# Attention and routed experts on one core: the first loads in half heads on two queues, wider idle products, and VectorE for the second pair's copies

## The chip, the cores and the metric

The kernel runs on one core of one Trainium2 chip. The metric is the device time of one execution in microseconds, as a median over runs. The profile below comes from one execution with the hardware profiler on; its times count from the start of the profiled span.

## The reference

Two blocks are chained. The first is windowed attention for 4 batches, 8 heads, 768 positions and a head size of 64; the second sends each of the 3072 resulting rows of 512 to one of 8 experts. All numbers are float32. Cut to what matters:

```python
scores = scale * np.matmul(q, k.transpose(0, 1, 3, 2))
is_global = pos[None, :] < int(n_global)               # n_global = 8
is_local = (rel >= 0) & (rel < int(n_local))           # n_local = 96
dist = np.where(is_global & ~is_local, float(n_local), np.abs(rel))
scores = np.where(is_global | is_local, scores - slopes * dist, -1e9)
a = np.exp(scores - max); a = a / sum(a)
x = (a @ v) laid out as 3072 rows of 512
expert_idx = argmax(cosine(x, expert_emb) / tau)       # the gate is the softmax value there
out[rows of e] = gate * (relu(x @ w1[e]) @ w2[e])      # 512 -> 1024 -> 512
```

`n_global` and `n_local` are inputs, so the kernel has to load these two numbers before it can build its table of bias factors.

## The kernel before, in words

**Attention.** A group is four heads of one batch, so there are eight groups; a group holds two pairs of heads. For a pair, `k` and `q` are loaded with positions on the partitions (`load_tokens`, L420, one DMA for a head) and turned on TensorE (`turn`, L455: three transposes into one PSUM bank, then copies to `kT` or `qT` by ScalarE, L457, L460 and L462). `turn(t, i)` takes half of `k` (i of 0 and 1) or half of `q` (i of 2 and 3). The 768 positions are cut into eight blocks of 96, each with the first 30 positions beside it as possible global columns. A unit is one block of a group: `score` (L480) makes its scores for four heads in two PSUM banks, `grow` (L486, ScalarE) takes the exponential, `weigh` (L493, VectorE) multiplies by the table, `attend` (L509 for the values, L519 for the sums) multiplies by `v`. A step has two units, so a group has four steps, and the attention of a step is issued one step later.

**The start.** All of group 0 is loaded at once. SyncE issues the first halves of `k` (L420, four DMAs of 96 KB), ScalarE those of `q`; then SyncE alone issues the second halves of `q`, the values (`load_v`, L426, four DMAs of 192 KB; L429, one of 30 KB for the global rows, which GpSimd spreads to the other blocks, L430), the second halves of `k`, two small loads for the router (L140, L142) and then group 1. The two numbers come in by two DMAs that GpSimd issues (`load_numbers`, L109). VectorE turns them into values (L112 to L117), builds the distances (`window_table`, L353 to L368), and ScalarE makes the table from them (L373, four instructions for four heads). VectorE also clears the five PSUM banks (L701). `busy(n)` (L706) issues n products of a matrix of ones, whose result nobody reads; a float32 product is two records in the trace. They stand ahead of the first turns and between them.

**What sets the order.** In this part the order on TensorE, ScalarE, VectorE and SyncE is the order of the program text, GpSimd's is the planner's. Each DMA of SyncE and ScalarE takes the next of eight semaphores in turn, so the issue of a DMA waits until the eighth DMA before it has landed. SyncE issues in order: what waits holds up all that follows.

**The rest.** After the eight groups come routing, gathers and the experts. The change doesn't touch them.

Of the kernel before, what the change touches and what calls it, by code (L numbers as in the profile page):

```python
# [10 lines left out]
I32 = mybir.dt.int32  # L11
# [9 lines left out]
P = 128  # L21
# [10 lines left out]
BLK = 96  # L32
GLB = 30
BAND = 32
ROWS = BLK + GLB
NB = 8
# [67 lines left out]
def load_numbers(k, n_global, n_local):  # L104

    nc, pool = k.nc, k.const
    raw = pool.tile([P, 2, 2], I32, name="raw")
    for i, ap in enumerate((n_global, n_local)):
        nc.gpsimd.dma_start(raw[:, i, :], ap.bitcast(I32).partition_broadcast(P))  # L109
    yield  # L110
    words = pool.tile([P, 2, 2], F32, name="words")
    nc.vector.tensor_copy(out=words[:], in_=raw[:])  # L112
# [264 lines left out]
def window_attention(k, ctx):  # L377
# [3 lines left out]
    nc, tc, NT, D, B, S, H, E = k.nc, k.tc, k.NT, k.D, k.B, k.S, k.H, k.E  # L381
# [18 lines left out]
    banks = [pa_p.tile([P, 512], F32, name="pa%d" % i) for i in range(5)]  # L400
    turn_of = [0]

    def bank():
        turn_of[0] += 1
        return banks[turn_of[0] % len(banks)]
# [8 lines left out]
        t.kT = kt_p.tile([P, NB, P], F32, name="kT", tag="kT")  # L414
        return t

    def load_tokens(eng, dst, src, b, a, r0, r1):

        for e in range(2):
            eng.dma_start(dst[:, r0:r1, e, :],  # L420
                          src[b, 2 * a + e].rearrange("(t p) d -> p t d", p=P)[:, r0:r1, :])

    def load_v(g, hs):
        for h in hs:
            src = k.v[g.b, 4 * g.m + h]
            nc.sync.dma_start(g.v[0:BLK, h], src.rearrange("(j r) d -> r j d", r=BLK))  # L426

        h0, h1 = hs[0], hs[-1] + 1
        nc.sync.dma_start(g.v[BLK:ROWS, h0:h1, 0], k.v[g.b, 4 * g.m + h0 : 4 * g.m + h1, 0:GLB].rearrange("h r d -> r h d"))  # L429
        nc.gpsimd.tensor_copy(out=g.v[BLK:ROWS, h0:h1, 1:], in_=g.v[BLK:ROWS, h0:h1, 0:1].to_broadcast([GLB, h1 - h0, NB - 1, D]))  # L430

    def new_group(b, m):
        g = Net()
# [6 lines left out]

    def load_part(g, p):
        if p < 2:
            load_tokens(nc.sync, g.pairs[p].k, k.k, g.b, 2 * g.m + p, 0, NT)
            load_tokens(nc.sync, g.pairs[p].q, k.q, g.b, 2 * g.m + p, 0, NT)
        else:
            load_v(g, (2 * p - 4, 2 * p - 3))

    def turn(t, i):  # L450

        src, half = (t.k, t.q)[i // 2], i % 2
        ps = bank()
        for r in range(3):
            nc.tensor.transpose(ps[:, r * P : (r + 1) * P], src[:, 3 * half + r, :, :], k.ident[:])  # L455
        if i < 2:
            nc.scalar.copy(out=t.kT[:, 4 * half : 4 * half + 4, 0:BLK],  # L457
                           in_=ps[:, 0 : 3 * P].rearrange("d (j c) -> d j c", c=BLK))
        else:
            nc.scalar.copy(out=t.qT[:, 3 * half * P : 3 * (half + 1) * P], in_=ps[:, 0 : 3 * P])  # L460
        if i == 0:
            nc.scalar.copy(out=t.kT[:, :, BLK:ROWS], in_=t.kT[:, 0:1, 0:GLB].to_broadcast([P, NB, GLB]))  # L462

    def score(u):

# [221 lines left out]
    first = groups[0]  # L687
    open_group(first)
    numbers = load_numbers(k, k.n_global, k.n_local)
    next(numbers)  # L690
    build_consts(k)
    for a in range(2):
        load_tokens(nc.sync, first.pairs[a].k, k.k, 0, a, 0, 3)
        load_tokens(nc.scalar, first.pairs[a].q, k.q, 0, a, 0, 3)
    warm = const.tile([P, 1], F32, name="warm")
    nc.scalar.activation(warm[:], k.ones[:, 0:1], AF.Exp)
    for a in range(2):
        load_tokens(nc.sync, first.pairs[a].q, k.q, 0, a, 3, NT)

    for ps in banks:  # L700
        nc.vector.memset(ps[:], 0.0)  # L701
    idle = bank()

    def busy(n):
        for _ in range(n):
            nc.tensor.matmul(idle[:, 0:64], lhsT=k.ones[:], rhs=k.ones[:, 0:64], start=True, stop=True)  # L706

    busy(8)
    load_v(first, range(4))
    for a in range(2):  # L710
        load_tokens(nc.sync, first.pairs[a].k, k.k, 0, a, 3, NT)
    emb = prep_expert_emb(k, k.emb_in, k.tau, tmp)
    next(emb)
    open_group(groups[1])
    for p in range(4):
        load_part(groups[1], p)
# [3 lines left out]
    next(table)  # L720
    next(numbers)
    next(table)
    check_numbers(k)
    build_route_consts(k)


# [870 lines left out]
def kernel(  # L1597
# [40 lines left out]
    with ExitStack() as moe:  # L1638
# [9 lines left out]
        with tc.manual_schedule(engines=ORDERED), ExitStack() as inner:  # L1648
            window_attention(n, inner)
# [130 lines left out]
```

## Time and profile before

| | |
|---|---|
| median of 3 runs | 523.97 us (522.73 to 524.47) |
| profiled execution, its own time | 524.56 us |
| its span | 522.8 us |
| TensorE busy, share of the span | 500.1 us, 96% |
| VectorE, ScalarE, GpSimd busy | 301.8 us, 197.2 us, 153.7 us |
| TensorE busy from 0 to 20 us | 15.55 us |
| HBM read, written | 61.66 MB, 17.16 MB |

The span runs from the first to the last instruction of the profiled execution, 1.8 us less than its own time. TensorE has work in nearly all of it. The first 20 us are the exception: its busy time there includes the idle products, and the loads of group 0 arrive in this time.

### The profile page before, as it was taken

How to read it: one execution, taken by the hardware profiler on the slowest of the kernel's cores; microseconds unless marked ns; L12 is line 12 of the kernel's file. 1: busy time of each engine (PE TensorE's matmuls, PEld its weight loads, DVE VectorE, ACT ScalarE, POOL GpSimd, SP SyncE). 2: the span in 40 equal slices, each digit the busy share in tenths (PEclk: the TensorE clock that was granted, in tenths of full speed). 3: DMA queues.
4: the chain of work that ended last, by engine and by line, in shares of the span. 5: the costliest groups of instructions: out<-in, count | busy, mean ns of one | idle time of the engine just before them, and what ended most of it. 6: DMA issues, size and time to landing. Idle time of an engine off the chain costs nothing.

```text
span 522.8 us, 13699 instructions
## 1 busy us (share of the span) xinstructions
PE 500.1 (96%) x5606; PEld 411.3 (79%) x5606; DVE 301.8 (58%) x602; ACT 197.2 (38%) x493; POOL 153.7 (29%) x169
## 2 busy tenths in 40 slices
PE   7899999999988998999999999999999999999995
PEld 7677887887765787859878759989889789859964
DVE  5647667666685664756745606765646644715531
ACT  4867766766653411302322312412312222302210
POOL 4221121442544235354240024144053050013023
PEclk9999999999998999999999999999999999999999
DMA  9999998898443346817573018357056064001001
GB/s 169 200 188 181 220 261 207 212 229 177 104 103 92 94 102 118 265 56 287 195 284 118 2 44 296 150 197 263 3 217 242 4 224 163 1 16 67 0 22 67
DMA packets 111421, 76.32 MB, mean 146 GB/s; under 512 B 87077, under 2 KB 95269, under 8 KB 111281
## 3 DMA queue, kind: packets, MB, share of 16 engines
q1 hardware_dynamic: 102769, 59.00, 42.1%
q0 software_dynamic: 6912, 15.26, 8.8%
q8 instruction: 63, 1.03, 0.9%
q14 instruction: 77, 0.63, 0.4%
q10 hardware_dynamic: 1600, 0.39, 0.3%
HBM read 61.66 MB, written 17.16 MB: 151 GB/s over the span
## 4 chain that ended last, share of the span: by engine, by line
PE 67%; issue 18%; DVE 3%; POOL 3%; ACT 3%; DMA 3%; SPq 1%; POOLq 1%; ACTq 0%; DVEq 0%
PE big L1303 17%; PE big L1108 9%; PE od L509 7%; PE pa L480 5%; PE work L1236 4%; PE od L519 3%; PE pa L455 3%; PE work L1108 3%; PE work L1249 3%; PE pa L671 2%; PE work L1017 2%; POOL out_dram L1255 2%; PE big L1279 2%; PE pa L582 2%; PE work L1027 1%
## 5 line engine op out<-in xcount | busy, mean ns | idle before, releaser
L493 DVE TENSOR_TENSOR ex<-ex,table 126x768 f32<-126x768 f32 x64 | 61.3, 964 | 45.1 <-ACT ex L486 44.9
L1315 DVE TENSOR_TENSOR hT<-big,hT 128x320 f32<-128x320 f32 (+4 forms) x70 | 39.4, 566 | 49.9 <-PE big L1303 49.7
L1255 POOL DMA_INDIRECT out_dram<-y_arm,tids x17 | 17.1, 1004 | 167.4 <-ACT y_arm L1238 121.1
L486 ACT ACTIVATE ex<-pa 126x384 f32<-126x384 f32 (+1 forms) x128 | 53.3, 477 | 24.4 <-PE pa L480 18.6
L1303 PE MATMUL big<-xT,w1t 128*128 128x160 f32 (+4 forms) x336 | 59.4, 330 | 1.1 <-issue 1.1
L1303 PEld LDWEIGHTS big<-xT,w1t 128*128 128x128 f32 x336 | 54.2, 190 | 3.9 <-issue 2.0
L991 POOL DMA_INDIRECT xg<-x_dram,idss x32 | 35.4, 1106 | 42.9 <-PE big L1303 21.5
L509 PE MATMUL od<-ex,v 126*64 126x192 f32 (+1 forms) x576 | 47.0, 309 | 0.0
L480 PE MATMUL pa<-qT,kT 64*32 64x128 f32 (+4 forms) x2048 | 41.0, 263 | 3.7 <-issue 3.5
L480 PEld LDWEIGHTS pa<-qT,kT 64*32 64x32 f32 (+1 forms) x2048 | 30.2, 105 | 16.7 <-issue 12.3
L257 POOL DMA_INDIRECT meta<-mt,slot x24 | 27.2, 1133 | 49.9 <-DVE rd L553 20.9
L509 PEld LDWEIGHTS od<-ex,v 126*64 126x64 f32 x576 | 35.3, 139 | 7.9 <-issue 3.8
L1303 PE MATMUL big<-xsum,fsum 128*128 128x160 f32 (+4 forms) x224 | 39.6, 330 | 0.0
L1020 ACT COPY xT<-work 128x256 f32<-128x256 f32 x56 | 18.1, 375 | 56.0 <-PE work L1017 55.3
L1303 PEld LDWEIGHTS big<-xsum,fsum 128*128 128x128 f32 x224 | 36.1, 190 | 1.2
L1236 PE MATMUL work<-w2t,hT 128*128 128x512 f32 x80 | 35.1, 594 | 0.0
L1108 PE MATMUL big<-wsum,hsum 128*128 128x256 f32 x136 | 31.1, 380 | 1.1 <-issue 0.6
L1317 ACT ACTIVATE hT<-hT 128x320 f32<-128x320 f32 (+4 forms) x42 | 21.6, 533 | 25.5 <-DVE hT L1315 25.3
L430 POOL COPY v<-v 30x896 f32<-30x896 f32 (+1 forms) x15 | 18.4, 1239 | 41.1 <-DMA v<-in_v_dram 28.9
L1108 PEld LDWEIGHTS big<-wsum,hsum 128*128 128x128 f32 x136 | 25.7, 190 | 5.6 <-issue 1.4
L1236 PEld LDWEIGHTS work<-w2t,hT 128*128 128x128 f32 x80 | 15.1, 190 | 17.7 <-issue 17.6
L1113 DVE TENSOR_TENSOR ptmp<-big,ptmp 128x256 f32<-128x256 f32 x16 | 6.7, 421 | 38.0 <-PE big L1108 20.0
(246 smaller groups left out, 899.8 us busy)
## 6 DMA issues: line engine op xcount, KB each, us to landing
w1t<-in_moe_w_dram SPq DMA_DIRECT2D x6, 2048.0 KB
w2t<-in_moe_w_dram SPq DMA_DIRECT2D x6, 2048.0 KB
v<-in_v_dram SPq DMA_DIRECT2D x32, 192.0 KB
x_dram<-xs SPq DMA_DIRECT2D x23, 256.0 KB
k<-in_k_dram SPq DMA_DIRECT2D x28, 192.0 KB
q<-in_q_dram SPq DMA_DIRECT2D x28, 192.0 KB
w1t<-in_moe_w_dram SPq DMA_DIRECT2D x32, 128.0 KB
w2t<-in_moe_w_dram SPq DMA_DIRECT2D x32, 128.0 KB
```

Of the source, the lines that this page charges most:

```text
L257: i = nc.gpsimd.indirect_dma_start(out=k.meta[:], out_offset=bass.IndirectOffsetOnAxis(ap=slot[:, t : t + 1], axis=0), in_=mt[:, t, :], in ...
L480: i = nc.tensor.matmul(u.sp[e][k0:k1, a * n + c0 : a * n + c1], lhsT=t.kT[rows, j, k0:k1], rhs=t.qT[rows, j * BLK + c0 : j * BLK + c1], st ...
L486: nc.scalar.activation(u.ex[:, e], u.sp[e][0:ROWS, 0 : 2 * u.n].rearrange("p (a c) -> p a c", a=2), AF.Exp, scale=k.scale)
L493: nc.vector.tensor_tensor(out=exv, in0=exv, in1=tab[:, :, 0 : u.n // BLK, :], op=ALU.mult)
L509: nc.tensor.matmul(g.od[a][e * D : (e + 1) * D, at : at + c1 - c0], lhsT=g.v[0:ROWS, 2 * a + e, u.j, :], rhs=u.ex[:, e, a, c0:c1], start=f ...
L991: i = k.nc.gpsimd.indirect_dma_start(out=xg[:], out_offset=None, in_=k.x_dram[0 : upto or k.N + 1, :], in_offset=bass.IndirectOffsetOnAxis ...
L1108: i = self.k.nc.tensor.matmul(ps, lhsT=x[:, f, :], rhs=w[:, f, :], start=f == 0 and not add, stop=True, skip_group_check=True)
L1236: nc.tensor.matmul(ps[:], lhsT=hT[:, f, j * P : (j + 1) * P], rhs=w2[:, f, :], start=i == 0, stop=i == k.NF - 1)
L1255: i = k.nc.gpsimd.indirect_dma_start(out=k.out.rearrange("t (i m) -> (t i) m", i=n), out_offset=bass.IndirectOffsetOnAxis(ap=ids, axis=0), ...
L1303: nc.tensor.matmul(to[f // 2][:, f % 2 * 256 : f % 2 * 256 + h], lhsT=x[:, l, f * P : (f + 1) * P], rhs=y[:, l, 0:h], start=not (add or f ...
L1315: nc.vector.tensor_tensor(out=to, in0=x, in1=z, op=ALU.add)
L1317: nc.scalar.activation(to, to, AF.Relu)
```

## The change

- The two numbers are loaded by one DMA on SyncE and one on ScalarE, as the first of each queue, and no longer by GpSimd.
- The first halves of `k` and `q` come in the order k, q of pair 0, then k, q of pair 1, with one head of each on SyncE and the other on ScalarE. Before, SyncE had all of `k` and ScalarE all of `q`.
- The values of group 0 are loaded in two parts: blocks 0 to 3 (four DMAs of 96 KB) and the global rows ahead of the second halves of `k`, blocks 4 to 7 behind them. The spread of the global rows on GpSimd has two parts too.
- The five clears of PSUM banks are gone.
- The idle products have 256 columns and no longer 64; there are 7, 3 and 2 of them, and no longer 8, 3 and 3.
- VectorE and no longer ScalarE makes the three copies of the second pair's first turns; `check_numbers` comes behind them.

```diff
-    for i, ap in enumerate((n_global, n_local)):
-        nc.gpsimd.dma_start(raw[:, i, :], ap.bitcast(I32).partition_broadcast(P))
+    for i, (eng, ap) in enumerate(((nc.sync, n_global), (nc.scalar, n_local))):
+        eng.dma_start(raw[:, i, :], ap.bitcast(I32).partition_broadcast(P))
...
-    def load_tokens(eng, dst, src, b, a, r0, r1):
+    def load_tokens(engines, dst, src, b, a, r0=0, r1=NT):
         for e in range(2):
-            eng.dma_start(dst[:, r0:r1, e, :],
-                          src[b, 2 * a + e].rearrange("(t p) d -> p t d", p=P)[:, r0:r1, :])
+            engines[e % len(engines)].dma_start(dst[:, r0:r1, e, :],
+                                                src[b, 2 * a + e].rearrange("(t p) d -> p t d", p=P)[:, r0:r1, :])
-    def load_v(g, hs):
+    def load_v(g, hs, j0=0, j1=NB):
...
-            nc.sync.dma_start(g.v[0:BLK, h], src.rearrange("(j r) d -> r j d", r=BLK))
+            nc.sync.dma_start(g.v[0:BLK, h, j0:j1], src.rearrange("(j r) d -> r j d", r=BLK)[:, j0:j1])
...
-    def turn(t, i):
+    def turn(t, i, copy=nc.scalar.copy):
...
-    for a in range(2):
-        load_tokens(nc.sync, first.pairs[a].k, k.k, 0, a, 0, 3)
-        load_tokens(nc.scalar, first.pairs[a].q, k.q, 0, a, 0, 3)
+    for a, t in enumerate(first.pairs):
+        load_tokens((nc.sync, nc.scalar), t.k, k.k, 0, a, 0, 3)
+        load_tokens((nc.sync, nc.scalar), t.q, k.q, 0, a, 0, 3)
...
-    for ps in banks:
-        nc.vector.memset(ps[:], 0.0)
     idle = bank()
     def busy(n):
-        for _ in range(n):
-            nc.tensor.matmul(idle[:, 0:64], lhsT=k.ones[:], rhs=k.ones[:, 0:64], start=True, stop=True)
-    busy(8)
-    load_v(first, range(4))
-    for a in range(2):
-        load_tokens(nc.sync, first.pairs[a].k, k.k, 0, a, 3, NT)
+        for i in range(n):
+            nc.tensor.matmul(idle[:, i % 2 * 256 : i % 2 * 256 + 256], lhsT=k.ones[:],
+                             rhs=k.ones[:].unsqueeze(1).to_broadcast([P, 2, P]), start=True, stop=True)
+    busy(7)
+    load_v(first, range(4), 0, NB // 2)
+    for a, t in enumerate(first.pairs):
+        load_tokens((nc.sync,), t.k, k.k, 0, a, 3, NT)
+    load_v(first, range(4), NB // 2, NB)
...
-    check_numbers(k)
     build_route_consts(k)
...
     busy(3)
-    turn(first.pairs[1], 0)
-    turn(first.pairs[1], 2)
+    turn(first.pairs[1], 0, nc.vector.tensor_copy)
+    turn(first.pairs[1], 2, nc.vector.tensor_copy)
     next(table)
-    busy(3)
+    check_numbers(k)
+    busy(2)
```

More of the change, by code (lines that the diff above doesn't have):

```diff
@@ L415, in new_pair @@
         return t
[L417 removed]
+    def load_tokens(engines, dst, src, b, a, r0=0, r1=NT):
         for e in range(2):
[L420 to L423 removed]
+            engines[e % len(engines)].dma_start(dst[:, r0:r1, e, :],
+                                                src[b, 2 * a + e].rearrange("(t p) d -> p t d", p=P)[:, r0:r1, :])
+    def load_v(g, hs, j0=0, j1=NB):
         for h in hs:
             src = k.v[g.b, 4 * g.m + h]
[L426 removed]
+            nc.sync.dma_start(g.v[0:BLK, h, j0:j1], src.rearrange("(j r) d -> r j d", r=BLK)[:, j0:j1])
         h0, h1 = hs[0], hs[-1] + 1
[L429 to L430 removed]
+        if j0 == 0:
+            nc.sync.dma_start(g.v[BLK:ROWS, h0:h1, 0], k.v[g.b, 4 * g.m + h0 : 4 * g.m + h1, 0:GLB].rearrange("h r d -> r h d"))
+        j0 = max(j0, 1)
+        nc.gpsimd.tensor_copy(out=g.v[BLK:ROWS, h0:h1, j0:j1], in_=g.v[BLK:ROWS, h0:h1, 0:1].to_broadcast([GLB, h1 - h0, j1 - j0, D]))
     def new_group(b, m):
@@ L442, in load_part @@
         if p < 2:
-            load_tokens(nc.sync, g.pairs[p].k, k.k, g.b, 2 * g.m + p, 0, NT)
-            load_tokens(nc.sync, g.pairs[p].q, k.q, g.b, 2 * g.m + p, 0, NT)
+            load_tokens((nc.sync,), g.pairs[p].k, k.k, g.b, 2 * g.m + p)
+            load_tokens((nc.sync,), g.pairs[p].q, k.q, g.b, 2 * g.m + p)
         else:
             load_v(g, (2 * p - 4, 2 * p - 3))
-    def turn(t, i):
+    def turn(t, i, copy=nc.scalar.copy):
         src, half = (t.k, t.q)[i // 2], i % 2
@@ L456, in turn @@
         if i < 2:
-            nc.scalar.copy(out=t.kT[:, 4 * half : 4 * half + 4, 0:BLK],
-                           in_=ps[:, 0 : 3 * P].rearrange("d (j c) -> d j c", c=BLK))
+            copy(out=t.kT[:, 4 * half : 4 * half + 4, 0:BLK],
+                 in_=ps[:, 0 : 3 * P].rearrange("d (j c) -> d j c", c=BLK))
         else:
-            nc.scalar.copy(out=t.qT[:, 3 * half * P : 3 * (half + 1) * P], in_=ps[:, 0 : 3 * P])
+            copy(out=t.qT[:, 3 * half * P : 3 * (half + 1) * P], in_=ps[:, 0 : 3 * P])
         if i == 0:
-            nc.scalar.copy(out=t.kT[:, :, BLK:ROWS], in_=t.kT[:, 0:1, 0:GLB].to_broadcast([P, NB, GLB]))
+            copy(out=t.kT[:, :, BLK:ROWS], in_=t.kT[:, 0:1, 0:GLB].to_broadcast([P, NB, GLB]))
     def score(u):
@@ L691, in window_attention @@
     build_consts(k)
-    for a in range(2):
-        load_tokens(nc.sync, first.pairs[a].k, k.k, 0, a, 0, 3)
-        load_tokens(nc.scalar, first.pairs[a].q, k.q, 0, a, 0, 3)
+    for a, t in enumerate(first.pairs):
+        load_tokens((nc.sync, nc.scalar), t.k, k.k, 0, a, 0, 3)
+        load_tokens((nc.sync, nc.scalar), t.q, k.q, 0, a, 0, 3)
     warm = const.tile([P, 1], F32, name="warm")
     nc.scalar.activation(warm[:], k.ones[:, 0:1], AF.Exp)
-    for a in range(2):
-        load_tokens(nc.sync, first.pairs[a].q, k.q, 0, a, 3, NT)
-    for ps in banks:
-        nc.vector.memset(ps[:], 0.0)
+    for a, t in enumerate(first.pairs):
+        load_tokens((nc.sync,), t.q, k.q, 0, a, 3, NT)
     idle = bank()
     def busy(n):
-        for _ in range(n):
-            nc.tensor.matmul(idle[:, 0:64], lhsT=k.ones[:], rhs=k.ones[:, 0:64], start=True, stop=True)
-    busy(8)
-    load_v(first, range(4))
-    for a in range(2):
-        load_tokens(nc.sync, first.pairs[a].k, k.k, 0, a, 3, NT)
+        for i in range(n):
[3 more added lines that the diff above has]
+    load_v(first, range(4), 0, NB // 2)
+    for a, t in enumerate(first.pairs):
+        load_tokens((nc.sync,), t.k, k.k, 0, a, 3, NT)
+    load_v(first, range(4), NB // 2, NB)
     emb = prep_expert_emb(k, k.emb_in, k.tau, tmp)
```

## The prediction

> **What bounds the kernel now.** The page's busy times come first: TensorE 96%, so only a stretch in which it idles or does nothing useful can be won, and the change edits the first 20 us. The chain that ended last, in order of time (start, length, what), shows whose work counts there:
>
> ```profile
> 1.89 5.11 DMA q<-in_q_dram
> 7.00 0.02 issue
> 7.02 0.34 SPq L426
> ...
> 12.03 4.60 DMA k<-in_k_dram
> 16.63 0.14 issue
> 16.76 0.52 PE pa L455 x3
> 17.28 1.45 PE od L509 x16
> 18.73 0.71 PE pa L480 x19
> 19.44 1.24 ACT ex L486 x3
> ```
>
> The start is a chain of loads, not of products: SyncE can't issue the first values (L426) before a first half of `q` has landed at 7.00, the second halves of `k` are behind the values in its queue and land at 16.63, and TensorE's turn at 16.76 waits for them. From 19.44 ScalarE is the bound until 26.8 (it is busy 5.97 of the 6.00 us from 20 to 26), from 27 TensorE. From 27 us to the end of attention the waits name no load of `k` or `q` ahead of TensorE, so a lead at 27 us is kept.
>
> Why do loads issued by 2.94 land at 7.0? Busy time by stretch (PE, PEld, DVE, ACT, POOL, then clock, DMA share, GB/s):
>
> ```profile
> 2.50:3.50 1.00, 1.00 (x5) 1.00 (x5) 0.94 (x2) 0.53 (x1) 0.97 (x5) 1.00 1.22 270
> 3.50:5.50 2.00, 2.00 (x11) 2.00 (x11) 0.94 (x4) 0.96 (x2) 1.86 (x10) 1.00 0.60 112
> 5.50:7.50 2.00, 2.00 (x12) 2.00 (x12) 0.84 (x5) 0.61 (x2) 1.83 (x16) 1.00 1.17 233
> ```
>
> With work queued, the rate falls from 270 to 112 GB/s and comes back. In the trace's packets the fall starts with the first packet of GpSimd's queue (the two numbers, 3.3 us) and ends with its last (6.0 us). That is coincidence in time, not proof.
>
> The timeline shows the other engines:
>
> ```profile
> 2.50 3.68 PE L706 MATMUL pa<-ones 128*128 128x64 f32 x16 [2.50 <-DVE pa L701]
> 5.97 0.85 PE L455 MATMUL pa<-ident,k 128*128 128x128 f32 x3
> 6.52 0.17 DVE L112 CAST words<-raw 128x4 f32<-128x4 int32 x1 [1.54 <-DMA raw<-in_n_local_dram]
> 10.06 0.56 DVE L368 TENSOR_TENSOR w_rel<-w_rel,w_t 128x384 f32<-128x384 f32 x1
> 10.71 1.76 ACT L373 ACTIVATE table<-w_rel 128x384 f32<-128x384 f32 x4
> 12.38 1.23 ACT L486 ACTIVATE ex<-pa 126x384 f32<-126x384 f32 x3
> 15.93 0.52 PE L455 MATMUL pa<-ident,k 128*128 128x128 f32 x3 [0.70 <-DMA k<-in_k_dram]
> 20.10 0.82 PE L455 MATMUL pa<-ident,q 128*128 128x128 f32 x6
> ```
>
> Pair 0's `k` landed at 4.17 and `q` at 4.45 (semaphore updates in the trace), yet the turn starts at 5.97: the idle products stand ahead of it. The first exponential waits until 12.38, behind a table that waits for the numbers. Group 1's second `q` landed at 19.94, and the turn at 20.10 takes it at once.
>
> **What the Trainium skill says.** "TensorE: Matmul & The Clock Gate", Part 1: the array runs at half clock until about a busy window of 3.4 us has passed, and windows run free of the kernel's start. The trace agrees: a transpose record lasts 421 ns before 9.5 us and 272 later, and the products' pace changes from 213 to 112 ns at 9.8 us. "DMA: Bandwidth & Descriptors", "Issuing engines are not separate DMA queues": a second issuing engine saves issue time only; here that is 0.49 us for 96 KB. The same page, "SWDGE vs HWDGE vs iDMA": software rings and hardware queues share the engines, which take turns between them; the dip above is consistent with that.
>
> **The change part by part.**
> *Clears* (five, 2.65 us of VectorE): gone. TensorE's first product waits only for `ones`, done at 1.08, so it starts at 1.1 and no longer at 2.50.
>
> *Idle products.* A warm record of 256 columns takes 216 ns start to start (L1108 in the trace); cold is twice that, 430. busy(7) is 14 records: 6.0 us cold. Before, 16 records took 3.47. When does the clock come on? Counting back windows of 3.41 from 9.82 gives edges at 6.41 and 2.99; the window between them held 64-column products, which fill half of the array time, and did not switch the clock. With 256 columns it is full, so I take 6.4. Ends: 4.5 with a lucky phase, 9.8 if the width doesn't matter. With 6.4: busy(7) ends at 6.8; two turns at 6 x 0.107 = 0.64 to 7.4; busy(3) 6 x 0.216 = 1.3 to 8.7; two turns to 9.35; busy(2) 0.86 to 10.2. Scores start at 10.2 against 10.47, a gain of 0.3 only (9.2 and 11.9 at the ends).
>
> *Numbers first.* Two more DMAs, one on each queue: 0.5 us of delay for the rest of each queue; ScalarE's fifth DMA now waits for the first number, with its table load and the copies (from 6.86 before) behind it, and 1.5 us of room. They should land near 3. The iotas on GpSimd come 1.3 us sooner (its two issues, 0.73 and 0.58, are gone), so L353 runs at 3.3 and the VectorE stretch of 4.1 us (6.52 to 10.62) ends near 7.8.
>
> *Copies.* ScalarE loses 0.48 + 0.39 + 0.47 = 1.34 us. VectorE gets three; a 128x384 copy from PSUM is 0.55 on VectorE (L525), so about 1.45 with the spread: from 9.2 to 10.7, where ScalarE finished at 10.59. Queued behind are `check_numbers` (0.5) and the first `weigh`, which is not due before 12. The table (1.76) runs at 8.6 to 10.4 and no longer at 10.71 to 12.47. So the first exponential starts when the first unit is scored, near 11.2 against 12.38: 1.2 us sooner.
>
> *Order of the loads.* Ahead of the second halves of `k` now lie 393 + 31 KB of values and not 786 + 31; at the 203 GB/s of 7.5 to 14 us that is 1.9 us. Without the dip another 1.5 or so. I estimate them at 12 to 13, against 16.63; TensorE asks for them near 13.5, so this wait is gone, and what is late next is bank and exponential on ScalarE. The first attention then starts near 14.9 (before 17.21), the scores of step 2 wait for ScalarE's copies, and ScalarE reaches step 2's exponentials near 17.4 against 19.42: **2.0 us**.
>
> *What that runs into.* The bytes up to group 1 are the same, but SyncE has 24 issues ahead of it and not 19: +5 x 0.5 = 2.5 us, against which its two waits (2.85 to 3.71 and 5.67 to 7.02, 2.2 us) should vanish. First issue of group 1 near 13.7, before 13.45; with less queued ahead of it, the second `q` should land near 18.5, before 19.94. TensorE would take it at 17.9, so it loses 0.6 there; but before, ScalarE came to step 3's exponentials at 24.88, 0.6 after their scores. So the lead stays at 1.9 to 2.0. GpSimd's spread of the first part (about 0.9 of the 1.98) has its rows by 10. The planner also puts one square root (0.88) ahead of the last spread of values at 134 us; that spread is used ten microseconds later, so it costs nothing.
>
> *Sum.* 524.56 - 2.0 = 522.6 for the profiled execution. That one lies 0.6 above the median, so the median goes to **522.0**.
>
> **The rivals.** (B) *The clock comes on at 9.8 as before.* For: the full window before 6.41 did not switch it. Then turns and products run cold, scores start at 11.9 and the first exponential is 0.1 late; but `k` is no longer waited for, and step 2's exponentials come at 18.4: 1.0 gained, 523.0.
> (C) *The dip stays*, because small packets on any queue cause it, or it had another cause. The halves of `k` still come 1.9 earlier, group 1 does not: 0.3 to 0.7 gained, 523.5.
> (D) *Slower: SyncE becomes the bound.* If its waits don't vanish, its five more issues put group 1 back by up to 2.5 us. The turn at 20.10 has 0.1 us of room, and all of TensorE's queue stands behind it. It decides from a first issue of group 1 at about 15.0: with 15.5, it lands at 22 and the loss is about 1.7: 525.7. Against it: the values were issued late only because of the landing at 7.00.
> (E) *More:* an early switch (4.5 to 5.4) starts the scores at 9.2 to 9.7, and step 2 gains 3 us: 521.0.
>
> **How the numbers follow.** Main case 0.52, B 0.15, C 0.10, D 0.13, E 0.10. A measurement of this kernel can tell about 0.3%, 1.6 us, from no change: the bound is 522.4. The main case (gain 1.2 to 2.6) gives 0.43 faster and 0.09 same; E is faster; B gives 0.04 and 0.11; C 0.01, 0.07 and 0.02; D 0.02 same and 0.11 slower. Sum: faster 0.58, same 0.29, slower 0.13. The range from 520.5 to 524.5 holds all but D and the far end of E.
>
> **What would show it.** After: first L706 at 1.1; L455 at half its record time before 8 us; L112 near 3.5; L373 before 9; first L486 near 11; no load ahead of a turn at step 1; the rate without a dip from 3.5 to 5.5; group 1's first `k` issued before 14. Wrong if the turn of group 1's `q` comes after 20, if the scores start after 11, or if L112 still stands at 6.

## The result, and the profile after

The changed kernel is slower: 529.18 us median (524.49 to 531.98, 20 runs) against 526.41 us (522.11 to 529.37, 20 runs) for the kernel before, a ratio of 1.0056 with a 95% interval of [1.0036, 1.0076]. That is 2.8 us lost where 2.0 were forecast as a gain. Its profiled execution took 529.62 us, with a span of 527.8 (before: 522.8). The profiled execution of before, 524.56 us, lies low among its 20 runs, so the two traces differ by more than the medians do. Ratios and means below leave out the few runs that lie over 1.5% above the fastest of their kernel.

Read the same views as before. First the timeline of the kernel after (start, length, engine, line; in brackets the idle time before and what ended it). The code behind the edits is two lines lower: L457 is the turn, L488 the exponential.

```profile
1.12 5.29 PE L706 MATMUL pa<-ones 128*128 128x256 f32 x14 [1.12 <-DVE ones L51]
...
4.57 3.18 SPq L420 DMA_DIRECT2D q<-in_q_dram  x5
...
4.83 0.17 DVE L112 CAST words<-raw 128x4 f32<-128x4 int32 x1 [1.74 <-DMA raw<-in_n_local_dram]
...
9.06 1.76 ACT L373 ACTIVATE table<-w_rel 128x384 f32<-128x384 f32 x4 [1.00 <-DVE w_rel L368]
...
10.86 1.25 ACT L488 ACTIVATE ex<-pa 126x384 f32<-126x384 f32 x3
...
14.86 0.52 PE L457 MATMUL pa<-ident,k 128*128 128x128 f32 x3 [1.11 <-DMA k<-in_k_dram]
...
16.27 0.98 SPq L420 DMA_DIRECT2D k<-in_k_dram  x2
...
20.27 0.52 PE L457 MATMUL pa<-ident,k 128*128 128x128 f32 x3 [1.54 <-DMA k<-in_k_dram]
...
23.26 1.51 PE L457 MATMUL pa<-ident,q 128*128 128x128 f32 x6 [2.47 <-DMA q<-in_q_dram]
```

Up to 10.86 the start is ahead of the old one: the first product at 1.12 (2.50), the table at 9.06 (10.71), the first exponential at 10.86 (12.38). From then on TensorE waits for loads. In the kernel before, group 1's first issue was this:

```profile
13.45 1.41 SPq L420 DMA_DIRECT2D k<-in_k_dram  x2
```

Now TensorE waits 1.1 us for the second half of `k`, group 1's first issue stands at 16.27 and no longer at 13.45, and the turn of group 1's `q` comes at 23.26 and no longer at 20.10, after waits of 1.54 and 2.47 us.

The stretches (busy time of PE, PEld, DVE, ACT, POOL; then clock, DMA share, GB/s), first the head as before, then the time around group 1's turns:

```profile
2.50:3.50 1.00, 1.00 (x4) 0.75 (x3) 0.36 (x1) 0.00 (x0) 0.93 (x5) 1.00 0.08 7
3.50:5.50 2.00, 2.00 (x7) 1.62 (x6) 0.56 (x4) 0.27 (x1) 1.83 (x17) 1.00 1.03 219
5.50:7.50 2.00, 2.00 (x13) 1.61 (x12) 1.90 (x7) 1.91 (x4) 0.18 (x2) 1.00 1.19 203
...
20.00:24.00 4.00, 1.26 (x7) 1.08 (x8) 1.81 (x4) 1.26 (x3) 0.27 (x1) 0.78 0.90 175
24.00:28.00 4.00, 4.00 (x31) 2.97 (x33) 0.56 (x1) 3.51 (x8) 0.00 (x0) 0.50 1.18 225
```

The last two stretches in the kernel before:

```profile
20.00:24.00 4.00, 4.00 (x91) 3.23 (x91) 3.17 (x6) 3.97 (x11) 0.00 (x0) 1.00 0.98 202
24.00:28.00 4.00, 3.39 (x84) 2.66 (x63) 1.67 (x4) 3.97 (x12) 0.14 (x1) 1.00 0.85 177
```

The dip of before (112 GB/s from 3.50 to 5.50) is gone, but there is a deeper one earlier: 7 GB/s from 2.50 to 3.50, where before moved 270. In the trace's packets, the two numbers are 256 packets of 8 bytes (128 for each number), from 1.8 to 4.4 us, and the first packet of `k` starts at 3.38 us (1.92 before). The numbers themselves land at 4.55 and 4.81. On GpSimd's queue, in the kernel before, the same two loads are 64 packets: 32 of 64 bytes and 32 of 4. The lower rows show the other loss: TensorE is busy for 1.26 of 4.00 us from 20 to 24 (4.00 before), and the granted clock is half afterwards. In the trace it is half from 22.3 to 29.1 us. (The clock column reads 1.00 wherever the trace holds no record of the clock. The first record is the switch to full clock, at 5.20 us here and 9.82 before, so the upper rows don't show the cold start.)

The chain that ended last, in order of time (start, length, what), for the first 26 us:

```profile
1.26 4.50 DMA k<-in_k_dram
5.76 0.02 issue
5.78 0.37 SPq L420
...
16.27 0.39 SPq L420
16.65 0.04 issue
16.70 0.54 SPq L420
...
17.87 5.30 DMA q<-in_q_dram
23.17 0.09 issue
23.26 2.15 PE pa L457 x9
25.41 2.12 PE od L511 x16
```

From 5.78 to 17.87 this chain holds nothing but SyncE's issues and the 0.04 us between them. (One of them, at 11.97, takes 1.40 us where its like take 0.49; what held it the trace doesn't say.) SyncE has become the bound of the start. Its two waits are still there; the waits of SyncE up to 24 us (line, what for, us in total, times, longest):

```profile
SPq L420 <- DMA raw<-in_n_global_dram: 1.8, 1, 1.8
SPq L420 <- DMA k<-in_k_dram: 0.8, 1, 0.8
```

And before:

```profile
SPq L426 <- DMA q<-in_q_dram: 1.3, 1, 1.3
SPq L420 <- DMA q<-in_q_dram: 0.9, 1, 0.9
```

That is 2.6 us, against the 2.2 of before. With five more issues (0.45 for the number, 2.1 for four of values) the sum is 13.45 + 2.5 + 0.4 = 16.35; the trace has 16.27.

### The profile page after: what moved, and what is told of

Same layout as the page of the kernel before. It is cut to its first block, busy times and chain, and to the rows that moved or that the text cites. A ratio compares the mean times of both kernels' runs of the same rounds, so it can differ in the third digit from the quotient of the medians.

```text
span 527.8 us, 13689 instructions
## 1 busy us (share of the span) xinstructions
PE 501.8 (95%) x5602; PEld 411.6 (78%) x5602; DVE 301.1 (57%) x600; ACT 196.9 (37%) x490; POOL 148.2 (28%) x168
## 3 DMA queue, kind: packets, MB, share of 16 engines
q0 software_dynamic: 6848, 15.26, 8.6%
## 4 chain that ended last, share of the span: by engine, by line
PE 70%; issue 17%; DMA 3%; POOL 3%; DVE 2%; SPq 2%; ACT 2%; POOLq 0%; ACTq 0%; DVEq 0%
PE big L1305 17%; PE big L1110 10%; PE od L511 7%; PE pa L482 5%; PE work L1238 4%; PE od L521 4%; PE pa L457 3%; PE work L1110 3%; PE work L1251 3%; PE pa L673 3%; PE work L1019 3%; POOL out_dram L1257 2%; PE big L1281 2%; PE pa L584 2%; PE work L1029 1%
## 5 line engine op out<-in xcount | busy, mean ns | idle before, releaser
L488 ACT ACTIVATE ex<-pa 126x384 f32<-126x384 f32 (+1 forms) x128 | 53.4, 477 | 26.4 <-PE pa L482 17.2
L993 POOL DMA_INDIRECT xg<-x_dram,idss x32 | 32.9, 1028 | 43.8 <-PE big L1305 17.6
L432 POOL COPY v<-v 30x896 f32<-30x896 f32 (+2 forms) x16 | 18.6, 1178 | 41.1 <-DMA v<-in_v_dram 25.9
```

The source lines that it names most:

```text
L488: nc.scalar.activation(u.ex[:, e], u.sp[e][0:ROWS, 0 : 2 * u.n].rearrange("p (a c) -> p a c", a=2), AF.Exp, scale=k.scale)
L993: i = k.nc.gpsimd.indirect_dma_start(out=xg[:], out_offset=None, in_=k.x_dram[0 : upto or k.N + 1, :], in_offset=bass.IndirectOffsetOnAxis ...
```

## The experiments

Three theories were open. **N**: the numbers at the heads of the two queues cost the start; its closer form, **P**, says that the number of their packets does. **V**: the values in two parts cost SyncE's issue time. **C**: neither matters much by itself, the half clock behind a late group 1 does. Some expectations below use further letters and say what they mean. Each ratio is to the kernel before, from runs of one comparison on one chip, with its 95% interval. Chip and hour differ between the comparisons: the kernel before has medians from 525.3 to 526.4 us in the earlier ones and 518.6 to 518.7 in the later, so times are to be compared by their ratios.

### One part of the change undone

The numbers on GpSimd's queue again:

```diff
-    for i, (eng, ap) in enumerate(((nc.sync, n_global), (nc.scalar, n_local))):
-        eng.dma_start(raw[:, i, :], ap.bitcast(I32).partition_broadcast(P))
+    for i, ap in enumerate((n_global, n_local)):
+        nc.gpsimd.dma_start(raw[:, i, :], ap.bitcast(I32).partition_broadcast(P))
```

> The changed kernel, with the two numbers loaded by GpSimd as before; all else as changed. Theory N (the numbers at the head of both hardware queues hold the start): the first k packets start near 2.0 us instead of 3.4, SyncE no longer waits for a number at its fifth issue, its first issue of group 1 comes near 14.5 instead of 16.27, and about half of the loss goes: 1.0 to 2.0 us less than the changed kernel. Theory V (the values in two parts alone fill SyncE's queue): the first packets come sooner, but group 1's first issue stays after 15.5 and the time stays within 1 us of the changed kernel.

Measured: 1.0015 [0.9981, 1.005]. The first packet of `k` is back at 1.905, group 1's first issue at 14.35, the turn of its `q` at 20.25; the old dip is back (130 GB/s from 3.50 to 5.50), the words at 6.45 and the first exponential at 12.46. So the start of group 1 is nearly that of before, and what the earlier numbers had gained is given back. The ratio fell as theory N said, though its interval still overlaps that of the changed kernel.

The values whole, ahead of the second halves of `k`:

```diff
-    load_v(first, range(4), 0, NB // 2)
+    load_v(first, range(4))
...
-    load_v(first, range(4), NB // 2, NB)
```

> The changed kernel, with the values of group 0 in one part (four DMAs of 192 KB) ahead of the second halves of k, as before. Theory V: four issues of 0.49 us fewer, group 1's first issue near 14.3 instead of 16.27, its second q lands near 21 instead of 23.2, no re-throttled clock, 2 to 3 us less than the changed kernel. Theory N: group 1's issue moves by less than 1 us, since the lag was made at the head of the queues; the time falls by under 1 us, and the second halves of k are waited for again (near 17).

Measured: 0.9997 [0.9977, 1.0018]. The first issue of group 1 falls from 16.27 to 13.99, the turn of its `q` from 23.26 to 21.56, although the first packet of `k` is as late as in the changed kernel (3.39). The price is that TensorE waits 2.29 us for `k` at 16.18, and the clock is half from 16.1 to 19.5. SyncE's issue and the ratio moved as theory V said, and the interval is clear of that of the changed kernel; the full clock that the theory expected didn't come.

The changed kernel with 19 more idle products, of 128 columns, in step 2, 7 of them ahead of group 1's first turn and 12 ahead of its second:

```diff
+        if s == 2:
+            for _ in range(7):
+                nc.tensor.matmul(k.free, lhsT=k.ones[:], rhs=k.ones[:], start=True, stop=True, skip_group_check=True)
...
```

> The changed kernel, with 19 more products of 128 columns in step 2 (7 ahead of group 1's first turn, 12 ahead of the second), whose result nobody reads: they fill the two waits of TensorE at 18.7 and 20.8 us (1.54 and 2.47). Theory C (most of the loss is not the wait but the half clock that the idle window brings, 22.3 to 29.1 us in the profile): the loads come as late as before, but the clock stays full, and the time falls by 2.0 to 3.5 us. Theory without C (the late load is all): no fall beyond 0.5 us, or up to 1 us more.

Measured: 1.0026 [0.9997, 1.0054]. The loads are as late (first issue of group 1 at 16.35, its `q` turned at 23.98), but the clock stays full; this is the stretch that ran at 0.50:

```profile
24.00:28.00 4.00, 4.00 (x99) 3.30 (x102) 0.95 (x2) 3.26 (x8) 0.00 (x0) 1.00 1.02 201
```

The first transposes of the embedding, a few microseconds behind these turns in TensorE's queue, come at 30.40; the changed kernel has them at 32.45 and the one before at 27.09. So in the profile the half clock is 2 of the 5.4 us lost by then, or a little more, since the filling itself held the turn for 0.4 us after its `q` had landed (23.56). In the medians it is about half of the loss (1.0056 to 1.0026), but the intervals overlap, and this one reaches below 1: that filling helps and that the late loads still cost is seen in the profile, and in the medians only as a tendency.

### One part of the change alone, on the kernel before

Only the values in two parts (`load_v` of the change, called for blocks 0 to 3 ahead of the second halves of `k` and for 4 to 7 behind them):

> The kernel before, with only the values of group 0 in two parts around the second halves of k. Theory V: four more issues push group 1's first issue from 13.45 to about 15.4, its second q lands near 21.5 instead of 19.94, TensorE waits 1 to 2 us at group 1's turns, and the kernel is 1 to 3 us slower than before. Theory N: the second halves of k land 2 us sooner and the time is the same or up to 1.5 us less than before.

Measured: 1.0041 [1.0019, 1.0064]. Group 1's first issue 15.24, and TensorE waits 0.43 and 1.30 us at group 1's turns. The later issue and the loss are as theory V says, with nothing else changed. The way from one to the other is shown in part only: in this profile the embedding's transposes come at 27.45, 0.4 us later than before, with a full clock up to there. Where the rest of the 2.2 us is lost the trace doesn't say.

Only the numbers on SyncE and ScalarE, as in the change's first hunk:

> The kernel before, with only the two numbers moved from GpSimd to the heads of SyncE's and ScalarE's queues. Theory N (256 packets of 8 bytes, 16 on each DMA engine, take the engines about 1.5 us wherever they stand, so at the head of the queues they delay everything): the first k packets start near 3.4 us instead of 1.9, the numbers land near 4.7, group 1's first issue comes 0.5 to 1.0 us later than 13.45, the time is the same to 1.5 us more. Theory S (the dip of the kernel before came from GpSimd's software queue, and hardware queues carry such packets for nothing): the first k packets start near 2.4, group 1 comes sooner, the time falls by 0.5 to 1.5 us.

Measured: 1.0032 [1.0008, 1.0055]. The stretches of this kernel:

```profile
1.80:3.50 1.70, 1.00 (x5) 1.01 (x5) 1.53 (x4) 0.00 (x0) 1.56 (x11) 1.00 0.07 6
3.50:5.50 2.00, 2.00 (x11) 2.00 (x11) 1.30 (x7) 0.13 (x1) 1.83 (x16) 1.00 1.05 224
```

6 GB/s up to 3.50, as in the changed kernel, and the first packet of `k` at 3.21. The words stand 1.55 us earlier (4.97), and that buys nothing: the first exponential is at 12.75, because the scores are now the late ones (11.55 for 10.47; in this execution the clock was full only from 15.15 us, so the packets are not the one reason). Here too the embedding's transposes, at 27.39, are only 0.3 us late, of the 1.7 lost in the medians.

Only the wide idle products (7, 3 and 2, no clears):

> The kernel before, with only the idle products changed (7, 3 and 2 of 256 columns for 8, 3 and 3 of 64) and the five clears of PSUM banks gone. Theory W (the wide products switch the clock on sooner): full clock at 4 to 7 us instead of 9.8, the first scores at 9.5 to 10.4, but TensorE then waits for the second halves of k just as before (16.6), so the time is the same within 0.3%. Rival: the clock was switched on early and then lost in the longer idle window ahead of 16.6 us, as in the profile of the kernel with the values in one part (half clock from 16.1 to 19.5): 1 to 2 us more.

Measured: 0.9968 [0.9946, 0.9989], the one part of the three that gains. The clock is full from 7.2 us and the embedding's transposes come at 26.20, 0.9 us sooner than before. But the 0.9 us don't come by an earlier start: the scores stand at 10.81 (10.47 before) and the first exponential at 12.57 (12.38). What came sooner is the landing of the last half of `k`, at 15.73 for 16.63, so that TensorE, which waited 1.0 us for these loads before, waits no more. Why they land sooner with other idle products no run shows; in one profile it can be chance.

What was left, the half heads on two queues together with VectorE's copies of the second pair:

> The kernel before with only the parts of the change that no run has tried alone: the first loads in half heads over both queues, and VectorE's copies for the second pair (with the counters' tables moved behind them). Numbers on GpSimd, values whole, narrow idle products. If the change is the sum of its parts, this is worth 0.56 - 0.41 = 0.15% in loss, within the noise of both: ratio 0.999 to 1.003. If VectorE's copies stand behind the table's chain that waits for the numbers (words at 6.5 us), the first exponential is near 12.4 to 12.9 as before and PE waits 0.5 to 1.4 us for a q copy. Group 1's first issue near 13.4 and its turns near 20.

Measured: 0.9992 [0.9969, 1.0016]. No measurable effect. Loss by values +0.41%, by numbers +0.32%, wide products -0.32%, the rest -0.08%: the four sum to +0.33%, with an uncertainty of about 0.45% from the four intervals, and the whole change measured +0.56%.

### Is it the number of packets?

First the changed kernel with the numbers on GpSimd and the values whole, behind the second halves of `k`, with only their global rows ahead of them:

```diff
-    load_v(first, range(4), 0, NB // 2)
...
-    load_v(first, range(4), NB // 2, NB)
+    load_v(first, range(4), "global")
+    load_v(first, range(4), "rest")
```

> The changed kernel with the numbers on GpSimd again and the values whole (four DMAs of 192 KB), issued behind the second halves of k, with their global rows ahead of them. Theory N+V (the loss is five more issues and the numbers at the head of the queues; the rest of the change is sound): group 1's first issue near 13.0, its second q lands near 19, no wait for the second halves of k (they land near 12), the first attention near 15, the transposes of the experts' embedding at 25.5 to 26.3 instead of 27.09 in the kernel before; 1 to 2 us less than before. Rival (the wide products or VectorE's copies cost by themselves): no better than the kernel before, though the loads come sooner.

Measured: 1.0001 [0.9974, 1.0029]. The first issue of group 1 fell to 13.19, but the first exponential went to 12.88: VectorE's copies of the second pair stand in its queue behind the table's instructions, which wait for the numbers (words at 6.89), and TensorE waits 1.42 us for the copy of `qT`. The gain of 1 to 2 us that theory N with V expected didn't come.

Then, on top of this, each number into one partition, and spread over 128 by a product with ones:

```diff
-    raw = pool.tile([P, 2, 2], I32, name="raw")
+    raw = pool.tile([1, 2, 2], I32, name="raw")
...
-        nc.gpsimd.dma_start(raw[:, i, :], ap.bitcast(I32).partition_broadcast(P))
+        nc.gpsimd.dma_start(raw[:, i, :], ap.bitcast(I32).partition_broadcast(1))
...
+    nc.tensor.matmul(k.spare[:, 0:2], lhsT=k.ones[0:1, :], rhs=one[:], start=True, stop=True)
+    num = pool.tile([P, 2], F32, name="num")
+    nc.vector.tensor_copy(out=num[:], in_=k.spare[:, 0:2])
```

> As the last, and the numbers are loaded into one partition only (one packet each instead of 128) and spread over the partitions by a product with ones on TensorE. Theory P (the cost of the numbers is their packet count): no dip in the DMA rate from 3.5 to 5.5 us, the first halves of pair 1 land near 5.5 instead of 7.5, group 1's loads come 1 to 1.5 us sooner than in the last kernel, the table starts near 9.5; 0.5 to 1.5 us less than the last. Rival (the dip has another cause, such as GpSimd's software queue as such): the dip stays and so does the time.

Measured: 0.998 [0.9959, 1.0]. The dip is gone, with the same queue and the same two DMAs, so it was the spread over 128 partitions that made it:

```profile
3.50:5.50 2.00, 2.00 (x6) 1.61 (x5) 0.36 (x1) 0.96 (x2) 1.86 (x10) 1.00 1.08 218
```

That the number of packets made it, theory P, is not shown: on GpSimd's queue the trace has 64 packets either way. In the kernel before, 32 of them have 64 bytes and take 13 to 380 ns each, the others 4 bytes; here all have 4 bytes and take 9 to 11 ns.

The first exponential is not sooner, though, but at 14.57, for a reason that no theory had:

```profile
10.41 1.68 POOL L434 COPY v<-v 30x1792 f32<-30x1792 f32 x1 [2.87 <-DMA v<-in_v_dram]
10.42 2.08 DVE L371 TENSOR_TENSOR w_rel<-w_rel,w_t 128x384 f32<-128x384 f32 x1
```

This VectorE instruction takes 0.56 us in the kernel before. The Trainium skill's "GPSIMD Engine Reference", key points, says that GpSimd shares its interfaces to SBUF with VectorE, which competes when an instruction has two inputs from SBUF; this one has two, and it ended only after GpSimd's copy had. The kernel before has a case too: the product with the table at 14.40 (L493, two inputs from SBUF) takes 2.17 us beside the copy from 13.78 to 15.76, and 0.96 alone. In the profile of this run with one partition the clock is also half, from 13.6 to 17.0; it fell in a wait of TensorE of 2.30 us.

The same on the changed kernel, with the two queues of the change kept:

> The changed kernel with one thing different: its two numbers are loaded, on the same two queues and at the same place, into one partition (one packet each in place of 128), and spread by a product with ones. If the packets' number is what the head pays for, the first packet of k moves from 3.38 us to about 2.0, the numbers land near 2.8 to 3.2 (4.55 and 4.81), SyncE's wait at its fifth issue goes from 1.83 us to under 0.6, and group 1's first issue from 16.27 to about 15: the values in two parts still put five issues and a landing ahead of it. Then group 1's second q lands near 21.7, its turns end at 21.5 to 22, and the ratio to before is about 1.001 to 1.004, as with the numbers on GpSimd (1.0015). If instead any small transfer ahead of k on a hardware queue costs the head its 1.5 us, the first packet stays over 3 us and the ratio at 1.004 to 1.008.

Measured: 0.9988 [0.9967, 1.001]; the changed kernel itself is at 1.0056. The head is repaired, yet SyncE is not:

```profile
3.00 0.25 DVE L112 CAST words<-raw 1x4 f32<-1x4 int32 x1
...
15.26 0.98 SPq L423 DMA_DIRECT2D k<-in_k_dram  x2
...
22.33 1.51 PE L460 MATMUL pa<-ident,q 128*128 128x128 f32 x6 [2.54 <-DMA q<-in_q_dram]
```

On these queues the two numbers are now two packets of 8 bytes where there were 256. The first packet of `k` is at 2.26 (3.38), the numbers are there at 3.00 (this is the "near 3" of the prediction), but group 1 is first issued at 15.26, because the values are still in two parts. In this execution the clock is half from 21.4 to 28.2.

### Putting the good parts together

The wide products and each number into one partition, first by GpSimd's queue and then by those of SyncE and ScalarE, all else as before:

> The kernel before with two things changed: the wide idle products (256 columns, 7, 3 and 2, no clearing of the banks) and the two numbers loaded into one partition by GpSimd's queue and spread over 128 by a product with ones. Everything else, ScalarE's copies of the second pair too, as before. If the number of the packets makes the dip (theory P, as the one-partition run with the whole change showed), the stretch from 3.50 to 5.50 us carries over 200 GB/s (112 before) and the second halves of k land about 1 us earlier than 13.92 to 16.63; group 1's first issue stays near 13.3, since SyncE waits for nothing there. Expected: clock on near 7.2, group 1's turns at 19 to 19.5, ratio to before 0.995 to 0.998, at or a little under that of the wide products alone (0.9968). If VectorE is again held by GpSimd's copy near 10.4, the first exponential moves from 12.4 to 14 and the gain is gone: ratio 0.999 to 1.001.

> The kernel before with the wide idle products and the two numbers loaded into one partition by the SyncE and ScalarE queues, ahead of k, spread by a product with ones: the pieces that the runs so far speak for, put together. If the packets' number is the cost, the numbers land near 3, the words stand on VectorE near 4 (6.52 before), there is no dip, the first exponential comes at 11 to 12, and group 1's first issue at 13 to 14. Expected ratio to before 0.994 to 0.998. If issue time decides (two issues more ahead of k on two queues, 0.05 to 0.1 us each, and the fifth issue waiting on the first), it loses up to 0.3 us against the same kernel with GpSimd's queue and reads 0.996 to 0.999.

Measured: 0.9964 [0.9946, 0.9982] and 0.9975 [0.9955, 0.9996]; the wide products alone had 0.9968. With GpSimd's queue the stretch from 3.50 to 5.50 carries 227 GB/s and group 1's first issue is at 12.27, but removing the dip adds nothing that these intervals can tell. On the queues of SyncE and ScalarE the words stand at 3.00, and the spread comes too late to use that, since its product has its place behind the first 14 records of the idle products:

```profile
6.67 0.38 PE L119 MATMUL pa<-one,ones 1*128 1x2 f32 x2
```

The changed kernel with both losing parts repaired (each number into one partition, values whole):

> The changed kernel with both suspected parts undone: each number one packet into one partition (same two queues), and the values whole in their old place. What is left of the change is the wide idle products, the half heads and VectorE's copies. If the loss is a sum of the packets (about 0.45% of the time) and the values in parts (about 0.45%), against a gain of 0.33% by the wide products, this reads 0.9967, between 0.995 and 0.9985; group 1's first issue near 13, its q turns near 19.5 without a wait over 0.6 us, and no half clock there. If the two are one cause (a late group 1 that either alone would cure), it reads as with one of them undone, 0.9985 to 1.000.

Measured: 0.9971 [0.9951, 0.999]. Group 1's first issue is at 12.45, the turn of its `q` at 19.38 with no wait for a load. The sum of two costs had foretold 0.9967, one common cause 0.9985 to 1.000: the sum is favoured, but against 0.9988 with one part repaired the intervals overlap.

### Does one profile stand for the others?

> The changed kernel once more, unchanged, to see how far its one profile stands for its executions. If the half clock after group 1's q is what costs, it is there again: q turn at 22.5 to 23.5, half clock for 6.8 us from about 22, first embedding transposes near 32. If it came in the first profile by chance, the clock stays full and they come near 29.

> The changed kernel with each number one packet, once more: its profiled execution (522.17 us) was near the top of its 22 (median 518.03). If most of its executions escape the half clock at group 1's q, this look has a full clock there or a q turn before 21.5, and embedding transposes at 27 to 29; if it is there again (31 to 32), the start does not explain why this kernel is level with the one before.

> The changed kernel with the values whole, once more: in its first profile group 1's q turn came at 21.56, half clock at 16.1 to 19.5, and embedding transposes at 28.55 with a median level with the kernel before. If the start repeats from execution to execution, it reads within 0.5 us of these; a spread over 1 us says that the landings of the first loads differ between executions.

The changed kernel again: 525.26 us, `q` of group 1 turned at 23.65, half clock from 24.3 to 27.7, embedding at 31.66. One partition again: 522.59 us, `q` at 22.22, half clock from 21.0 to 27.8, embedding at 31.31. Values whole again: 517.88 us, `q` at 23.06 where the first profile had 21.56, embedding at 29.78 for 28.55. In these comparisons the kernel before has a median of 518.72. So landings and what follows them move by over 1 us between executions. The first issue of group 1 repeats within 0.25 us (16.43 and 16.27; 15.04 and 15.26; 14.10 and 13.99), so SyncE's lateness is no chance. The half clock is there each time too, but 3.4 us long in one execution and 6.8 in another of the same kernel.

The times of single executions and their mean granted clock tell more than these profiles. In 213 runs of the kernel before in four comparisons, a straight line through time against clock has a slope of 333 to 398 us for 1.0 of clock (339 to 462 with the five slowest, which are left out). A half clock for 6.8 us lowers the mean by 6.8 / 2 / 527 = 0.0065, so a run with 0.994 or more had none of that length.

| kernel | mean clock over its runs | runs at 0.994 or more | ratio |
|---|---|---|---|
| before (four comparisons) | 0.9954 to 0.9969 | 176 of 213 | 1 |
| after | 0.9899 | 3 of 20 | 1.0056 |
| after, waits filled | 0.9950 | 10 of 14 | 1.0026 |
| after, numbers by GpSimd | 0.9942 | 8 of 13 | 1.0015 |
| after, values whole | 0.9930 | 7 of 20 | 0.9997 |
| after, one partition per number | 0.9939 | 14 of 22 | 0.9988 |
| after, both repaired | 0.9947 | 16 of 22 | 0.9971 |
| before, values in two parts | 0.9940 | 11 of 22 | 1.0041 |
| before, numbers by SyncE and ScalarE | 0.9953 | 14 of 18 | 1.0032 |
| before, wide products | 0.9961 | 14 of 18 | 0.9968 |

The clock of after is 0.0055 to 0.0070 lower than that of before (the clocks of the 20 runs of before beside it are not on record), which at these slopes is 1.8 to 2.8 us, most of the 2.8 lost. The mean doesn't say where in a run the half clock lay. Nor is the clock the whole account: with the values whole it is 0.9930, and the kernel is level with the one before. The table fits with an oddity: the kernel with one partition per number shows a start nearly as late as that of after in both of its profiles (embedding at 31.53 and 31.31), but both (clock 0.990 and 0.989) are among its low ones. Most of its runs had no stretch of that length; none of them was profiled, so this is not shown. The table is a correlation over runs, not an experiment; the run with the filled waits is the experiment, and it agrees in direction.

## Why the prediction was wrong

The forecast was the main case with 522.0 us, and its rival D happened: SyncE became the bound. By its own steps:

**Right in its times: the idle products and the clears.** TensorE started at 1.12 (said: 1.1). The clock was full at 5.2 us in this execution (said: 6.4, with ends of 4.5 and 9.8), the scores started at 10.01 (10.2). Alone, this part measured 0.32%, some 1.7 us, where the prediction gave it 0.3 us; in its profile the gain came by loads of `k` that landed sooner and not by earlier scores, so the size is not explained. The point where the clock comes on was between 4.0 and 7.2 in the kernels with wide products, and differed between executions of one kernel (5.2 and 7.2 for after), which agrees with what the prediction took from the Trainium skill, "TensorE: Matmul & The Clock Gate", Part 1: windows that run free of the kernel's start.

**Right, but smaller: the table and the first exponential.** L373 at 9.06 (said: 8.6), first exponential at 10.86 (11.2). ScalarE's step-2 exponentials came at 18.36: 1.1 us gained of the 2.0, since TensorE waited for `k`.

**Failed: "They should land near 3."** The price of the numbers was set at two issues, 0.5 us of delay. On the queues of SyncE and ScalarE they were 256 packets (64 on GpSimd's), took the engines for 2.6 us, landed at 4.55 and 4.81, and put the first packet of `k` back by 1.46 us. The prediction had itself tied the old dip to the packets of the numbers, and then moved these loads to the head of the queues that everything waits for without pricing them there. Alone this costs 0.32%; with one partition per number they landed by 3.00 and cost nothing measurable.

**Failed: "its two waits (2.85 to 3.71 and 5.67 to 7.02, 2.2 us) should vanish."** The other term, five issues at 0.5 us, was right (2.5). But the waits were 2.6 us. The first issue of group 1 stood at 16.27 and not at 13.7. Even with the head repaired they were 1.6 us and the issue at 15.26; rival D had put the point of decision at 15.0.

**Failed: the second halves of `k` "at 12 to 13".** They landed at 14.34, 14.72, 15.13 and 15.57. With the late head and 12 SyncE issues of 0.5 us each from 5.78 on, the last of the four was issued only at 11.97. So the last half came 1.1 us sooner than before (16.63), where 3.6 to 4.6 had been estimated.

**Not priced: the clock behind a late group 1.** Rival D counted lateness alone, 1.7 us from a landing at 22. The landing was 23.17, and the idle time in front of it halved the clock for 6.8 us. The prediction knew the clock's rule for the start and didn't ask what its own bad case would do to it later. The Trainium skill, "TensorE: Matmul & The Clock Gate", "HAM oscillation — how this bites in real kernels", describes just this, a wait for a DMA that spans a window and leaves the next products cold. It speaks of idle gaps over about 3.4 us; here the longest gap was 2.47, and the 3.41 us ahead of the switch at 22.27 held 0.52 us of TensorE work. The measurement decides: a nearly idle window was enough.

**The chances.** D had 0.13 against a main case of 0.52. Its mechanism was complete but for the clock; the reason given against it, that the values were issued late only because of the landing at 7.00, treated the landing as something that the change removes. The change put its own packets ahead of that very landing.

**Still open.** Whether the packets and the values in two parts are two costs that add or share the half clock as one; the last runs favour the sum without settling it. Why after's loss in later stages varies: half-clock stretches of 3.4 us between 149 and 218 us stand in 11 of the 18 profiles, that of before among them. How the values in two parts cost 2.2 us in the medians when their profile is 0.4 us behind at 27 us. And why the wide idle products gain.

## What to carry to other kernels

Before moving a small load to the head of a queue, count its packets on that queue and not its bytes: a number spread to 128 partitions was 128 of them on the queues of SyncE and ScalarE, and everything behind waited. When an issuing engine works in order, cost each split of a load as one more issue for all that is queued behind, and take a wait off the sum only when the thing it waits for has been shown to come sooner. Where a change can make TensorE idle for most of 3.4 us, add to its lateness the half clock that follows.

## What was not expected of the hardware

- 256 packets of 8 bytes, 128 for each number, took from 1.8 to 4.4 us. If they are spread evenly over the 16 DMA engines, that is 16 on each, an estimated 0.16 us a packet, while each record itself lasts 7 to 9 ns. The rate on the engines fell to 7 GB/s.
- The granted clock went to half after 3.41 us with 0.52 us of work in it, and stayed there for 6.8 us although TensorE was busy from 23.26 on; the first of the two windows held idle time up to 23.26, the second none, and then it came back. Seven of the 18 profiles have such a half clock before 30 us. Counted in steps of 3.41 us from each one's switch to full clock, the step ahead of it held 0.52 to 1.29 us of TensorE work, and no other step at full clock up to 40 us held less than 1.90. The half clock stayed for a second step where its first held 2.21 to 2.82 us of work (four profiles) and ended after one where that held 3.23 to 3.41 (three). This fits with one kernel showing 3.4 us in one execution and 6.8 in another. It is no fixed threshold: between 149 and 218 us the clock also fell after steps with 1.14 to 2.17 us of work.
- Idle products of 64 columns had the full clock on at 9.1, 9.6, 9.8 and 15.2 us in the four kernels with them, those of 256 columns at 4.0 to 7.2 in the other 14 profiles. The narrow ones started later, at 2.50 and not at 1.1 us; no run separates the width from the start.
- A VectorE instruction with two inputs from SBUF took 2.08 us and not 0.56 beside a copy on GpSimd; another, in the kernel before, 2.17 and not 0.96.
